# Attention startup: bias rows strided over partitions, a one-step maximum for the bias, first loads reordered

## The chip, the cores and the metric

The kernel runs on one core of a Trainium2 chip. The metric is the device time of one execution in microseconds. The kernel before takes 820.88 us (median of three runs, 820.48 to 823.38). Rows of the trace come from one profiled execution, which took 827.75 us, 826.0 of it between its first and last instruction (the span).

## The reference

Attention with a learned position bias, then two mixtures of experts. Only attention matters here; q, k and v have the shape (2 batches, 8 heads, 576 rows, 64).

```
scores = (q @ k^T) / 8
rel    = pos[:, None] - pos[None, :]
x      = log1p(|rel|) / log1p(max(pos_i, 1))        # 576 x 576
h      = max(x[..., None] @ w1 + b1, 0)             # 32 hidden units
bias   = h @ w2                                     # one 576 x 576 plane per head
attn   = softmax(scores + bias) ; out = attn @ v
```

The bias does not depend on the batch, so each row block of it serves both batches. The result is reshaped to 1152 tokens of 512 and goes through a dense mixture of 4 experts (every token, weighted by domain_probs) and a routed one of 8.

## The kernel before

**Tiles.** Attention is cut into nine units u: units 0 to 7 are 128 query rows of one batch (batch u % 2, rows from 128 * (u // 2)), unit 8 is the last 64 rows of both. A unit has eight heads; a step n is one head of one unit, n = 8 u + h, 72 steps in all. What is called head n below is the step with that n. The bias is made in five blocks of query rows (`blk`), four of 128 rows and one of 64 that is stored twice, for the two halves of unit 8; a block has eight pieces T of 16 rows (block 4 has four).

**A bias piece.** `bias_r` (L287) makes four row tiles r (tt = 0 to 3) of 128 x 576: the partitions are 4 query rows x 32 hidden units. Each is one instruction, on VectorE, ScalarE or GpSimd as the letters in `AT` and `RE` say: with log for the table `lm` of log1p(|rel|), shifted per row: max(log * w1 / psi_i, -b1) on VectorE and GpSimd, relu(log * w1 / psi_i + b1) on ScalarE; the constant that the first form leaves out is put back from `bconst`. `bias_mm` (L303) multiplies with a block-diagonal w2 on TensorE, `bias_out` (L315) evicts the two PSUM halves with ScalarE into bo (128 x 576: 16 rows x 8 heads) and SP sends bo to the 16 partitions 16 T to 16 T + 15 of the bias block; in block 4 two DMAs send it to both halves.

**Other helpers.** `load_q`, `load_k`, `load_v` issue loads on SP. `split` (L134) makes a high and a low part on GpSimd, two instructions; `k_split` and `split_q` use it. `q_trans` and `k_trans` transpose on TensorE, `k_out` (L203) copies a transposed k piece out of PSUM, q_trans's result is copied by ScalarE and then twice by SP (qt<-qt, 64 partitions each). `v_scale` finds a power of two for v of both batches, `v_mul` scales v, `v_hi` and `v_lo` split it.

**Order.** All is written out by hand inside `manual_schedule`: every engine and every DMA queue works in program order. L500 to L519: first loads, splits of q and k. L534 to L556: ten steps T that make block 0, with k's transposes of batch 0 and the first scores between. L557 to L568: splits of batch 1's k and three of its five passes `k_pass` (transposes and copies). From L574: steps n = -2 to 77, each with the transposes of head n, soft_max of head n + 2 on VectorE (L344), exp of head n + 1 on ScalarE (L354), the high part of the transposed e on ScalarE and the low part on VectorE, scores of head n + 3, and the product with v of head n - 2. Bias pieces of the next blocks are woven in (`group`); the last two k passes come in steps -2 and -1. Block 4's pieces are evicted from about n = 45 on.

**PSUM.** The transposes of e and of k share one pool of two buffers (`ps_et`).

Of the kernel before, what the change touches and what calls it, by code (L numbers as in the profile page):

```python
# [59 lines left out]

@with_exitstack
def attn_moe_moe_kernel(ctx, tc, q, k, v, w1, b1, w2, dp, mw1, mw2, wg, wog, ew1, ew2, cst, lmc, out):
# [173 lines left out]
    def v_scale(p, tag):  # L236
        pt = p.tile([128, 2, 128], F32, tag=tag, name="vtp")
        for b in range(2):
            dve.tensor_reduce(out=vmx[:, b:b + 1], in_=vt["raw"][:, b].rearrange("p n d -> p (n d)"), axis=AX.X, op=ALU.max,
                              apply_absolute_value=True)  # L240
            yield
        for b in range(2):
            pe.transpose(pt[0:1, b, :], vmx[:, b:b + 1], idn)
        dve.tensor_reduce(out=vma, in_=pt[0:1], axis=AX.X, op=ALU.max)
        pe.matmul(pt[:, 0, 0:2], lhsT=onr, rhs=vma, start=True, stop=True)
        yield
        dve.tensor_scalar(out=vP[:, 0:2], in0=pt[:, 0, 0:2], scalar1=1e-30, scalar2=None, op0=ALU.max)
        dve.tensor_scalar(out=vP[:, 0:2].bitcast(I32), in0=vP[:, 0:2].bitcast(I32), scalar1=0x7F800000, scalar2=None, op0=ALU.bitwise_and)
        dve.reciprocal(vR, vP[:, 0:2])
        for b in range(2):  # L250
            dve.tensor_copy(vP[64 * b:64 * b + 64, 2:3], vP[64 * b:64 * b + 64, b:b + 1])
        yield
# [1025 lines left out]
```

## Time and profile before

| | |
|---|---|
| median of three runs | 820.88 us |
| profiled execution, own time / span | 827.75 / 826.0 us |
| TensorE busy | 755.2 us (91%) |
| VectorE busy | 500.1 us (61%) |
| ScalarE busy | 470.2 us (57%) |
| GpSimd busy | 373.4 us (45%) |
| DMA | 160.18 MB, mean 194 GB/s |

In the rows further down PE is TensorE, DVE is VectorE, ACT is ScalarE, POOL is GpSimd and SPq is the queue of SyncE from which DMAs are issued. A name such as bias<-bo says what an instruction writes and reads; [3.51 <-DMA bias<-bo] says that the engine sat idle for 3.51 us and what ended that. The DMA share is the mean busy share of the core's 16 DMA engines and can go over 1 where packets overlap. [...]

### The profile page before, as it was taken

Reading aid. Unit: us, or ns where it says so; the run is one execution under the profiler, and the core shown is the slowest. Engines: PE = TensorE matmul, PEld = TensorE weight load, DVE = VectorE, ACT = ScalarE, POOL = GpSimd, SP = SyncE. Lnnn points to the kernel's source line nnn. Section 1 sums busy time; section 2 is a strip of 40 time slices with the busy share of each in tenths; the row PEclk is TensorE's granted clock in tenths of the full one; section 3 lists DMA queues with packets and bytes.
Section 4 is the critical chain, followed back from the end, with each engine's and each line's share of the span. In section 5 each row is a group of like instructions: output and inputs, shape, how many; then the busy total and the mean of one; then the engine's idle time right before and its main releaser. Section 6 shows DMA issues by size and latency. Waiting matters only on the chain. (4 is left out here: it accounts for less than half of the span.)

```text
span 826.0 us, 16298 instructions
## 1 busy us (share of the span) xinstructions
PE 755.2 (91%) x6305; PEld 482.9 (58%) x6305; DVE 500.1 (61%) x1120; ACT 470.2 (57%) x683; POOL 373.4 (45%) x265
## 2 busy tenths in 40 slices
PE   1777999997898999999999999999999789999994
PEld 0344777776786555555555555555555477667771
DVE  4979999986878565565555555554567373333220
ACT  1646899985674667667667667766663132222220
POOL 7737566562380555555555555555543103112110
PEclk9999999998999999999999999999999899999998
DMA  8944545599353567564846567573527738999340
GB/s 224 158 60 79 97 97 102 106 170 142 67 151 117 220 242 252 223 255 152 294 167 237 217 234 251 217 271 117 215 112 294 309 129 321 409 408 360 107 158 16
DMA packets 75039, 160.18 MB, mean 194 GB/s; under 512 B 20364, under 2 KB 28812, under 8 KB 74958
## 3 DMA queue, kind: packets, MB, share of 16 engines
q1 hardware_dynamic: 68832, 144.52, 55.7%
q0 software_dynamic: 4528, 14.47, 5.3%
q8 instruction: 51, 0.84, 0.4%
q10 hardware_dynamic: 1598, 0.11, 0.1%
q14 instruction: 30, 0.25, 0.1%
HBM read 116.32 MB, written 39.34 MB: 188 GB/s over the span
## 5 line engine op out<-in xcount | busy, mean ns | idle before, releaser
L494 POOL TENSOR_TENSOR ring<-wraw,ring 128x1024 f16<-128x1024 f32 x64 | 136.2, 2129 | 118.7 <-ACT wraw L491 102.6
L723 DVE SCALAR_TENSOR_TENSOR h<-hps,h 128x384 f16<-128x384 f32 x96 | 53.2, 557 | 146.4 <-ACT h L722 146.4
L718 PE MATMUL hps<-xt,wt 128*128 128x384 f16 x384 | 126.0, 328 | 2.2 <-DVE h L723 1.8
L720 PE MATMUL hps<-xt,wt 128*128 128x384 f16 x384 | 126.0, 328 | 0.0
L719 PE MATMUL hps<-xt,wt 128*128 128x384 f16 x384 | 126.0, 328 | 0.0
L459 DVE TENSOR_REDUCE wm<-wraw 128x1 f32<-128x1024 f32 x96 | 116.0, 1209 | 0.0
L491 ACT ACTIVATE wraw<-wraw,wR 128x1024 f32<-128x1024 f32 x91 | 104.5, 1148 | 3.0
L735 PE MATMUL yps<-wt,h 128*128 128x512 f16 x264 | 100.1, 379 | 0.0
L736 PE MATMUL yps<-wt,h 128*128 128x512 f16 x264 | 100.1, 379 | 0.0
L737 PE MATMUL yps<-wt,h 128*128 128x512 f16 x264 | 100.1, 379 | 0.0
L722 ACT ACTIVATE h<-hps 128x384 f16<-128x384 f32 x96 | 46.7, 487 | 88.5 <-PE hps L720 84.6
L494 POOL TENSOR_TENSOR wt<-wraw,wt 128x1024 f16<-128x1024 f32 x31 | 66.1, 2132 | 63.3 <-ACT wraw L491 63.0
L486 ACT ACTIVATE ring<-wraw,wR 128x1024 f16<-128x1024 f32 x64 | 73.0, 1141 | 21.5 <-DVE wR L475 18.8
L296 DVE TENSOR_SCALAR r<-lm,s,nb 128x576 f32<-128x576 f32 x89 | 75.8, 899 | 0.0
L335 PE MATMUL sc<-kt,qt 128*128 128x288 f32 x320 | 62.8, 321 | 13.6 <-DVE mn L344 7.3
L1036 PE MATMUL l<-xb,wb 128*128 128x128 f16 x1248 | 72.8, 219 | 2.5 <-DMA wb<-wdr 2.5
L1036 PEld LDWEIGHTS <-wb 128*128 128x128 f16 x1248 | 70.7, 98 | 6.4 <-DMA wb<-wdr 3.3
L1055 PE MATMUL l<-wb,xb 128*128 128x512 f16 x312 | 69.5, 379 | 0.8 <-ACT o L1059 0.8
L344 DVE CUSTOM_DVE_ANT_0 ns<-sc,bias 128x576 f32<-128x576 f32 x72 | 54.3, 754 | 24.6 <-PE sc L335 13.0
L1044 DVE SCALAR_TENSOR_TENSOR xb<-l,xb 128x512 f16<-128x512 f32 x26 | 17.6, 691 | 80.1 <-ACT xb L1043 80.1
L296 POOL TENSOR_SCALAR r<-lm,s,nb 128x576 f32<-128x576 f32 x20 | 45.7, 2285 | 42.7 <-PE bp L311 42.7
L1060 POOL DMA_INDIRECT out_x<-o,g x13 | 13.2, 1016 | 108.4 <-ACT o L1059 93.5
(246 smaller groups left out, 1459.2 us busy)
## 6 DMA issues: line engine op xcount, KB each, us to landing
wb<-wdr SPq DMA_DIRECT2D x104, 512.0 KB
wraw<-in_moe_w SPq DMA_DIRECT2D x84, 512.0 KB
wdr<-ring SPq DMA_DIRECT2D x64, 512.0 KB
bias<-bo SPq DMA_DIRECT2D x40, 288.0 KB
wraw<-in_moe_w POOLq DMA_DIRECT2D x12, 512.0 KB, 5.5
qt<-qt SPq DMA_DIRECT2D x40, 128.0 KB
ydr<-y POOLq DMA_DIRECT2D x9, 258.0 KB, 4.1
q<-in_q SPq DMA_DIRECT2D x8, 256.0 KB
```

The lines of the kernel that those rows point to most:

```text
L296: (dve if on == "v" else pool).tensor_scalar(out=r, in0=src, scalar1=sc, scalar2=nb1, op0=ALU.mult, op1=ALU.max)
L459: dve.tensor_reduce(out=wm[:, w_col(x), k:k + 1], in_=wraw[x][:, k], axis=AX.X, op=ALU.max, apply_absolute_value=True)
L486: act.activation(out=hi, in_=t, func=AF.Copy, scale=R)
L491: act.activation(out=t, in_=t, func=AF.Copy, scale=R)
L494: pool.tensor_tensor(out=lo, in0=t, in1=hi, op=ALU.subtract)
L718: pe.matmul(ps, lhsT=w[:, k, 0, fs], rhs=xt[:, c, 0, k, :], start=(k == 0), stop=False)
L719: pe.matmul(ps, lhsT=w[:, k, 0, fs], rhs=xt[:, c, 1, k, :], start=False, stop=False)
L720: pe.matmul(ps, lhsT=w[:, k, 1, fs], rhs=xt[:, c, 0, k, :], start=False, stop=(k == 3))
L735: pe.matmul(acc[m][t], lhsT=hh, rhs=w[:, f // 2, 0, ws], start=(f == 0), stop=False)
L736: pe.matmul(acc[m][t], lhsT=hh, rhs=w[:, f // 2, 1, ws], start=False, stop=False)
L737: pe.matmul(acc[m][t], lhsT=hl, rhs=w[:, f // 2, 0, ws], start=False, stop=(f == 7))
L1036: pe.matmul(ps[f // 4][:, f % 4, :], lhsT=w[:, k, a, f * 128:f * 128 + 128], rhs=xs[:, b, k, :], start=(k == 0 and f % 4 == 0 and i == 0), ...
```

## The change

**Rows strided.** Piece T of a block of 128 rows now holds rows T, T + 8, T + 16, ... instead of 16 adjacent rows (`row0`, and log1p's table shifted by 8 per group of rows), and one DMA writes every eighth partition from T on. In block 4 a piece goes out in four DMAs, each of 64 partitions of bo to eight partitions.

**One maximum.** log is multiplied by w1 once, in place (704 of its 1152 columns at the start, 448 after block 0). A row tile is then max(log * w1, -b1 * psi_i): one operation, with an accumulator output (`accum_out`) on VectorE and without on GpSimd; ScalarE adds a bias per partition. The factor 1 / psi_i moves to the eviction, as its scale operand.

**First loads.** w1, b1, w2's block-diagonal form, the reordered tables and domain_probs come from the host inside the constants; the first loads are log's 704 columns on SP and 342 columns of constants on ScalarE's queue, then q 0, k of batch 0 and two pieces of k of batch 1. The rest (`bulk`) follows one by one in the steps T.

**v and k.** v's factor is found per batch, without a transpose. v of batch 0 is loaded in the steps T, v of batch 1 behind block 0. v of batch 0 gets its high part from ScalarE, in steps -1 and 0. All five k passes of batch 1 run in steps -1 to 3, behind the product with v; all copies of them and more of batch 0's go to ScalarE. v of batch 1 is scaled in step 4.

```diff
+def row0(blk, T, tt):
+    return blk * 128 + T + 32 * tt if blk < 4 else 512 + 2 * T + tt // 2 + 32 * (tt % 2)
...
-        (dve.tensor_copy if x and not b else act.copy)(o, pt)
+        (dve.tensor_copy if x and not b and a < 2 else act.copy)(o, pt)
...
-        src, sc = lm[:, 575 - 4 * t:1151 - 4 * t], s1[:, t:t + 1]
-        if on != "a":
-            (dve if on == "v" else pool).tensor_scalar(out=r, in0=src, scalar1=sc, scalar2=nb1, op0=ALU.mult, op1=ALU.max)
+        r0 = row0(blk, T, tt)
+        src = lm[:, 575 - r0:1151 - r0]
+        if on == "v":
+            dve.tensor_scalar(out=r, in0=src, scalar1=nbp[:, t:t + 1], scalar2=None, op0=ALU.max, op1=ALU.max,
+                              accum_out=rmx[:, rb[1]:rb[1] + 1])
+        elif on == "p":
+            pool.tensor_scalar(out=r, in0=src, scalar1=nbp[:, t:t + 1], scalar2=None, op0=ALU.max)
         else:
-            act.activation(out=r, in_=src, func=AF.Relu, scale=sc, bias=b1c)
+            act.activation(out=r, in_=src, func=AF.Relu, bias=bps[:, t:t + 1])
...
-            act.activation(out=bo[:, z * 288:z * 288 + 288], in_=pt, func=AF.Identity, bias=bconst[:, w:w + 1])
-        for p0 in ([16 * T] if blk < 4 else [16 * T, 64 + 16 * T]):
-            sp.dma_start(out=bias_t[blk][p0:p0 + 16], in_=bo)
+            act.activation(out=bo[:, z * 288:z * 288 + 288], in_=pt, func=AF.Identity, bias=bconst[:, w:w + 1],
+                           scale=cs[:, C_INV + blk * 8 + T:C_INV + blk * 8 + T + 1])
+        if blk < 4:
+            sp.dma_start(out=bias_t[blk][T:128:8], in_=bo)
+            return
+        for x in range(2):
+            for p0 in (0, 64):
+                sp.dma_start(out=bias_t[blk][p0 + 2 * T + x:p0 + 64:8], in_=bo[64 * x:64 * x + 64])
...
-        act.dma_start(out=w1c, in_=rep4(w1, 1))
-        act.dma_start(out=b1c, in_=rep4(b1, 1))
-        sp.dma_start(out=cs, in_=cst[:, 0:C_N])
-        sp.dma_start(out=lm, in_=lmc)
-        act.dma_start(out=w2s, in_=rep4(w2, 8))
+        sp.dma_start(out=lm[:, 448:1152], in_=lmc[:, 448:1152])
+        act.dma_start(out=cs[:, 0:C_UT], in_=cst[:, 0:C_UT])
         load_q(0)
         for a in (0, 1, 2):
             load_k(0, a)
+        for a in (2, 0):
+            load_k(1, a)
...
+        dve.tensor_scalar(out=nbp, in0=cs[:, C_RP:C_RP + 144], scalar1=b1c, scalar2=-1.0, op0=ALU.mult, op1=ALU.mult)
+        act.activation(out=bps, in_=nbp, func=AF.Copy, scale=-1.0)
+        dve.tensor_scalar(out=lm[:, 448:1152], in0=lm[:, 448:1152], scalar1=w1c, scalar2=None, op0=ALU.mult)
...
+        bulk = [lambda: load_k(1, 1), lambda: load_q(1), lambda: load_v(0, 0), lambda: load_v(0, 1), lambda: load_v(0, 2),
+                lambda: sp.dma_start(out=lm[:, 0:448], in_=lmc[:, 0:448]), lambda: None, lambda: load_v(1, 0)]
...
-            if T in (5, 7):
-                next(vs)
-            if T == 8:
-                qk(0)
+        for a in (1, 2):
+            load_v(1, a)
...
-        k_pass(4, 0, 1)
...
             if n == -2:
+                v_scale(0)
                 v_mul(0)
-                for a in range(5):
-                    v_hi(0, a, pool)
-                    v_lo(0, a)
-                    if a == 2:
-                        split_q(1)
...
+            if n in (-1, 0):
+                for a in ((0, 1, 2), (3, 4))[n + 1]:
+                    v_hi(0, a, act)
+                    v_lo(0, a)
+                if n == 0:
+                    split_q(1)
...
-                    bias_r(1, n + 2, tt, "vvvv"[tt] if n == -1 else "vavv"[tt])
+                    bias_r(1, n + 2, tt, "vavv"[tt])
...
-                k_pass(n + 4)
...
+            if -1 <= n < 4:
+                k_pass((4, 0, 1, 2, 3)[n + 1])
+            if n in (1, 2):
+                v_max(1, n - 1)
             if n == 2:
+                v_pow(1)
+            if n == 4:
+                v_scale(1)
                 v_mul(1)
```

## Rows read from the trace of the kernel before

**Rows 1.** The page's 40 slices, TensorE's busy tenths.

```profile
PE   1777999997898999999999999999999789999994
```

**Rows 2.** Windows: length, busy us (instructions) of PE, PEld, DVE, ACT, POOL; PEclk, share, GB/s.

```profile
0.00:10.00 10.00, 0.00 (x0) 0.00 (x0) 0.45 (x2) 1.28 (x1) 4.19 (x14) 1.00 0.74 187
10.00:20.00 10.00, 2.99 (x12) 0.96 (x16) 7.53 (x10) 1.74 (x4) 9.69 (x9) 1.00 0.96 257
...
16.00:18.00 2.00, 0.63 (x4) 0.22 (x4) 2.00 (x2) 1.20 (x2) 1.92 (x2) 1.00 1.11 334
...
20.00:50.00 30.00, 24.02 (x188) 11.58 (x188) 28.76 (x34) 16.32 (x31) 16.51 (x13) 1.00 1.01 149
...
110.00:130.00 20.00, 19.95 (x257) 15.76 (x256) 18.77 (x42) 18.46 (x35) 11.87 (x8) 1.00 0.51 101
```

**Rows 3.** Timeline, GpSimd and VectorE at the start: start us, us, instruction, count.

```profile
3.54 0.29 POOL L510 CAST idb<-cs 128x128 bf16<-128x128 f32 x1 [2.64 <-DMA cs<-in_cst]
...
11.43 3.12 DVE L525 COPY w2b<-w2s 32x8 f32<-32x8 f32 x4 [2.17 <-DMA w2s<-in_w]
...
15.82 14.69 DVE L296 TENSOR_SCALAR r<-lm,s,nb 128x576 f32<-128x576 f32 x11
...
41.26 1.55 DVE L296 TENSOR_SCALAR r<-lm,s,nb 128x576 f32<-128x576 f32 x3
...
60.20 7.10 DVE L296 TENSOR_SCALAR r<-lm,s,nb 128x576 f32<-128x576 f32 x6
```

**Rows 4.** Timeline: last eviction of block 0 and the first soft_max (head 0).

```profile
46.12 0.89 ACT L320 ACTIVATE bo<-sc,bconst 128x288 f32<-128x288 f32 x2 [1.26 <-PE sc L311]
...
53.28 0.76 DVE L344 CUSTOM_DVE_ANT_0 ns<-sc,bias 128x576 f32<-128x576 f32 x1 [3.51 <-DMA bias<-bo]
```

**Rows 5.** Windows: the hole in the traffic, its end, and a qt transfer.

```profile
22.00:24.00 2.00, 1.27 (x7) 0.18 (x2) 2.00 (x3) 1.25 (x2) 1.92 (x3) 1.00 0.06 16
...
50.50:51.00 0.50, 0.50 (x4) 0.50 (x3) 0.00 (x0) 0.11 (x1) 0.00 (x0) 0.50 0.20 18
...
74.50:75.50 1.00, 0.95 (x15) 0.71 (x11) 1.00 (x4) 1.00 (x3) 0.63 (x1) 1.00 0.88 203
```

**Rows 6.** Timeline of VectorE: soft_max of heads 10, 18, 26, 42 and 58.

```profile
90.27 0.74 DVE L344 CUSTOM_DVE_ANT_0 ns<-sc,bias 128x576 f32<-128x576 f32 x1
...
109.78 0.76 DVE L344 CUSTOM_DVE_ANT_0 ns<-sc,bias 128x576 f32<-128x576 f32 x1
...
129.32 0.76 DVE L344 CUSTOM_DVE_ANT_0 ns<-sc,bias 128x576 f32<-128x576 f32 x1
...
168.39 0.76 DVE L344 CUSTOM_DVE_ANT_0 ns<-sc,bias 128x576 f32<-128x576 f32 x1
...
217.40 0.76 DVE L344 CUSTOM_DVE_ANT_0 ns<-sc,bias 128x576 f32<-128x576 f32 x1
```

**Rows 7.** The dip: a qt issue, the wait for it (timeline), and two windows.

```profile
185.95 0.50 SPq L165 DMA_DIRECT2D qt<-qt  x1
...
197.97 1.06 PE L335 MATMUL sc<-kt,qt 128*128 128x288 f32 x3 [4.23 <-DMA qt<-qt]
...
188.00:198.00 10.00, 5.75 (x76) 4.45 (x74) 5.77 (x12) 6.76 (x13) 4.57 (x3) 0.94 1.05 148
198.00:203.00 5.00, 5.00 (x37) 4.58 (x39) 2.04 (x6) 1.20 (x2) 0.00 (x0) 0.50 1.17 145
```

**Rows 8.** ScalarE's groups by form: shapes, count, busy us, mean ns; idle time before.

```profile
L354 ACT ACTIVATE e<-ns,mn 128x576 f32<-128x576 f32 x72 | 56.4, 783 | 0.3 <-DVE mn L344 0.2
L367 ACT ACTIVATE eth<-etp 128x512 f16<-128x512 f32 x72 | 43.2, 600 | 27.0 <-PE etp L361 27.0
L320 ACT ACTIVATE bo<-bp,bconst 128x288 f32<-128x288 f32 x64 | 30.2, 505 | 19.8 <-PE bp L311 18.1 <-issue 1.3
L298 ACT ACTIVATE r<-lm,b1c,s 128x576 f32<-128x576 f32 x35 | 30.2, 869 | 0.0
L209 ACT CAST kt<-ktp 128x512 fp32r<-128x512 f32 x12 | 7.2, 622 | 2.7 <-PE ktp L200 2.5
```

More of the change, by code (lines that the diff above doesn't have):

```diff
@@ L33 @@
 C_ID = 144
-C_UT = C_ID + 128
+C_W1 = C_ID + 128
+C_B1 = C_W1 + 1
+C_WB = C_B1 + 1
+C_INV = C_WB + 32
+C_UT = C_INV + 36
 C_IOTA = C_UT + 128
@@ L42 @@
 C_IOP = C_N
-C_ALL = C_IOP + 128
+C_DP = C_IOP + 128
+C_ALL = C_DP + 36
 NE = 3
@@ L234, in init_v, with v_max, v_pow, v_scale @@
             pool.memset(z[64 * e:64 * e + 64, :, :, 0, e, 64:65], 1.0)
[L236 to L252, printed above, removed]
+    def v_max(b, x):
+        raw = vt["raw"][:, b].rearrange("p (x n) d -> p x (n d)", x=2)
+        dve.tensor_reduce(out=vm2[:, x:x + 1], in_=raw[:, x], axis=AX.X, op=ALU.max, apply_absolute_value=True)
+    def v_pow(b):
+        m = vmx[:, b:b + 1]
+        dve.tensor_reduce(out=m, in_=vm2, axis=AX.X, op=ALU.max)
+        dve.tensor_scalar(out=m, in0=m, scalar1=1e-30, scalar2=None, op0=ALU.max)
+        dve.tensor_scalar(out=m.bitcast(I32), in0=m.bitcast(I32), scalar1=0x7F800000, scalar2=None, op0=ALU.bitwise_and)
+        dve.tensor_copy(vpb[:, b:b + 1], m)
+    def v_scale(b):
+        pt = ps_t.tile([128, 128], F32, tag="t", name="vpp")
+        pe.matmul(pt, lhsT=vpb[:, b:b + 1].to_broadcast([128, 128]), rhs=idb, start=True, stop=True)
+        dve.tensor_reduce(out=vP[:, b:b + 1], in_=pt, axis=AX.X, op=ALU.max)
+        dve.reciprocal(vR[:, b:b + 1], vP[:, b:b + 1])
+        dve.tensor_copy(vP[64 * b:64 * b + 64, 2:3], vP[64 * b:64 * b + 64, b:b + 1])
     def v_mul(b):
@@ L540, in attn_moe_moe_kernel @@
                     bias_r(0, T, tt, "a" if tt in AT[T % 2] else "v")
-            if 1 <= T < 9:
+            if T == 8:
+                for x in range(2):
+                    v_max(0, x)
+                v_pow(0)
+                qk(0)
+            if T:
                 bias_mm(0, T - 1)
                 bias_out(0, T - 1, len(AT[(T - 1) % 2]))
-            if 1 <= T < 4:
-                load_v(1, T - 1)
-            if T == 2:
+                bulk[T - 1]()
+            if T == 1:
                 q_trans(0, 0)
-            if 3 <= T < 8:
+            if 2 <= T < 7:
                 for g in range(2):
-                    k_trans(0, T - 3, g, ps_et, "et")
+                    k_trans(0, T - 2, g, ps_et, "et")
             if T == 4:
                 q_trans(0, 1)
-            if T in (5, 7):
-                next(vs)
-            if T == 8:
-                qk(0)
+        for a in (1, 2):
+            load_v(1, a)
+        sp.dma_start(out=cs[:, C_UT:C_N], in_=cst[:, C_UT:C_N])
+        dve.tensor_scalar(out=lm[:, 0:448], in0=lm[:, 0:448], scalar1=w1c, scalar2=None, op0=ALU.mult)
         for a in (4, 0, 1, 2, 3):
             k_split(1, a)
-        for _ in vs:
-            pass
         def k_pass(*pieces):
@@ L667, in attn_moe_moe_kernel @@
                 split_q(8)
-                dpr = dp.rearrange("(b t) e -> b t e", b=2)
-                for b in range(2):
-                    sp.dma_start(out=pr[:, b:8:2, :], in_=dpr[b, 0:512].rearrange("(k p) e -> p k e", p=128))
-                    sp.dma_start(out=pr[64 * b:64 * b + 64, 8, :], in_=dpr[b, 512:576])
+                sp.dma_start(out=pr, in_=cst[:, C_DP:C_DP + 36].rearrange("p (u e) -> p u e", e=4))
             if n == 70:
@@ L1226, in attn_moe_moe_kernel, with constants @@
                     pass
[L1229 removed]
+def constants(w1, b1, w2, dp):
     i = np.arange(S, dtype=np.float32)
     c = np.zeros((128, C_ALL), np.float32)
[L1232 to L1234 removed]
+    psi = np.log1p(np.maximum(i, np.float32(1.0)))
+    at = np.array([[row0(t // 32, t // 4 % 8, t % 4) + 8 * g for t in range(144)] for g in range(4)])
+    c[:, C_RP:C_RP + 144] = np.repeat(psi[at], 32, axis=0)
+    inv = (1.0 / psi)[at].reshape(4, 36, 4).transpose(2, 0, 1).reshape(16, 36)
+    c[:, C_INV:C_INV + 36] = np.repeat(inv, 8, axis=0)
+    c[:, C_ID:C_ID + 128] = np.eye(128)
+    for b in range(2):
+        d = dp.reshape(2, S, 4)[b]
+        c[:, C_DP:C_DP + 36].reshape(128, NU, 4)[:, b:8:2] = d[0:512].reshape(4, 128, 4).transpose(1, 0, 2)
+        c[64 * b:64 * b + 64, C_DP + 32:C_DP + 36] = d[512:576]
+    c[:, C_W1] = np.tile(w1.reshape(32), 4)
+    c[:, C_B1] = np.tile(b1.reshape(32), 4)
+    for g in range(4):
+        c[32 * g:32 * g + 32, C_WB + 8 * g:C_WB + 8 * g + 8] = w2
     c[:, C_UT:C_UT + 128] = np.triu(np.ones((128, 128)), 1)
```

56 lines of the change are left out of this document (19 added, 37 removed).

## The prediction

> **What bounds the kernel now.** I read the 40 slices first, then busy time in windows, then the timeline of the first 90 us. The PE line of the slices is full nearly everywhere except at its left edge and in a dip near 200 us [rows 1]; the windows say the same in numbers: TensorE is busy 19.95 of 20 us in the middle of attention [rows 2], so whatever only makes VectorE, ScalarE or GpSimd cheaper there is worth nothing. All that this change touches lies in two places: the time before attention runs at its own pace, and the dip.
>
> The pace: VectorE's soft_max of heads 18 and 26 start at 109.78 and 129.32, and head 10 at 90.27, 19.5 us before head 18 [rows 6]. So 19.54 us per 8 heads, and the kernel is "on the line" from head 10 on. What comes before is a startup of 90 us. Its hinge is the first soft_max (head 0) at 53.28: VectorE had stood idle 3.51 us, for the last DMA of the bias of block 0, although ScalarE had written that piece near 47.0 [rows 4]. The DMA engines were full: 1.01 share from 20 to 50 us at only 149 GB/s, against 257 from 10 to 20 [rows 2]. VectorE itself starts its bias rows only at 15.82, behind small loads (w2s came at 11.43) and 3.12 us of copies of w2 [rows 3], and then needs 14.69 us for 11 of them while GpSimd splits q and k; three of them take 1.55 us once GpSimd is idle [rows 3].
>
> **The change part by part.** All times are of the profiled execution (span 826.0, own time 827.75); the median of three runs is 820.88, so 6.9 us lower, and the difference is carried over at the end.
>
> *First loads and small copies.* Gone: three ScalarE DMAs and SP's load of all constants and all of lm (805 KB ahead of q), five VectorE copies, two GpSimd memsets. In their place 360 KB of lm (704 columns) on SP and 175 KB of constants on ScalarE's queue, side by side. The constants landed at 3.54 before, ahead of lm [rows 3]; I take 4.0 for both now, then nbp, the scaling of lm (704 columns, about as long as one bias row), w2r on GpSimd, the cp matmul and its two copies: first bias row at about 6, 10 us earlier.
>
> *Bias rows as one maximum.* The 24 VectorE rows of block 0 lose the multiplication and get an accumulator output. The trace has no such instruction. Bounds: 0.52 us (three in 1.55) and 1.34 us (11 in 14.69) [rows 3], the first without and the second with GpSimd at work. I take 0.70, near the soft_max instruction, which also writes an accumulator and is 0.76 long for the same 576 columns [rows 4], and which does not stretch. [...] 24 x 0.70 = 17 us, and two k copies: VectorE would be through the block at about 25. ScalarE has 8 rows of 0.87, 16 evictions of 0.505, eight copies of k of up to 0.62 (three of them taken over from VectorE) and two of q [rows 8]: 7 + 8 + 5 + 1 = 21 us, with its waits for the matmuls between, last eviction at about 28 (47.0 before). GpSimd's splits start about 1.5 us earlier than before, with q, and stay just ahead of the transposes. The scale operand on the eviction I cost at nothing: the instruction is the same.
>
> *DMA: what is ahead of the last bias piece.* Now the queue is late next. Ahead of the last piece lie: first loads (lm, constants, q 0, k of batch 0, two pieces of k of batch 1) 2583 KB; then the bulk loads spread over the steps (last k piece, q 1, v of batch 0, rest of lm) and four qt copies, 2661 KB; and eight bias pieces of 288 KB. Moved behind it: v of batch 1, 1152 KB. The first 10 us moved 1870 KB (187 GB/s) and after that 257 GB/s held [rows 2]: first loads through at 10 + 713/257 = 12.8, the rest another 10.4. A bias piece before: from 20 to 50.5 us, less the hole at 22 to 24 [rows 5], less 2166 KB of other data at 257 GB/s (8.4 us), 20.2 us for eight, 2.5 us each (115 GB/s). After, strided over partitions: nothing here writes 16 strided rows. Bounds: 2.5 us, and 1.1 us at 257 GB/s. I take 1.42, the rate of qt, which writes 64 partitions (203 GB/s at 0.88 share) [rows 5]; 8 x 1.42 = 11.4. Sum 12.8 + 10.4 + 11.4 = 34.6. From the end of traffic (50.5, [rows 5]) to the soft_max before there were 2.8 us; the same again gives head 0 at 37.4 instead of 53.3: **-16 us**. Bounds -7 (2.5 us a piece) and -22 (the queue keeps up and ScalarE's chain decides, 28 + 3 = 31). SP also issues the bulk loads behind evictions that it must wait for; since its backlog is never empty from 10 us on, I cost that at nothing; without the backlog it would be about 1 us.
>
> *From head 0 to the line.* Before, head 10 came 37.0 us after head 0 [rows 4, 6]. VectorE gets lighter: in step -1 six bias rows took 7.10 us [rows 3] and now five take 3.5; step -2 has four as before; some 4 us saved. ScalarE gets heavier: four of the k passes (two copies of 0.62 each [rows 8]), which ran before head 0 or in steps -2 and -1, now run one each in steps 0 to 3, and v's copies, that GpSimd made, in steps -1 and 0 (four like an exp of 0.78 or a little less, two of half the size). ScalarE's work by durations [rows 8]: step -1: exp 0.78, v 2.0, bias row 0.87, evictions 1.0, short k copies 0.7, together 5.4; likewise 5.1, 3.6, 4.1 and 4.0 in steps 0 to 3, 22.2 in all. Two evictions of 0.505 take 0.89 together [rows 4], so 0.12 goes off for each of the 36 instructions: 18 us, from the first evictions of block 1 at about +7 to +25, where step 4 begins. Added wait: the two transposes of a pass share two PSUM buffers with the transposes of e, so the second waits for a ScalarE copy or the next VectorE split; behind it on TensorE stand the next head's transposes, and ScalarE waits for those. A copy and half a pass of transposes, 0.8 us a pass, 4 us in all: step 4 at +29, and four heads more at 2.44 bring head 10 to +39: **+2 us**. Bounds: -3 (VectorE's gain alone counts) and +6 (the wait costs twice that). v of batch 1 is scaled in step 4 instead of 2; GpSimd has six steps for its halves until head 8's product needs them.
>
> *The dip.* Head 42 to head 58 took 49.0 us where two periods are 39.1 [rows 6]. [...] Block 3's pieces get quicker, so less stands in the queue when block 4 begins. But block 4's four steps issue four DMAs of 144 KB to eight partitions each instead of two of 288 KB. I take **-3 us**, between 0 (block 4 as slow as before) and -8 (no wait, no slow clock). [...]
>
> *At nothing:* block rows on TensorE's line (GpSimd's shorter rows, VectorE's fixed 0.70: TensorE covers them), the long reductions of v in halves (VectorE waits for the queue then anyway), four loads of domain_probs as one.
>
> Sum: -16 + 2 - 3 = -17. 827.75 - 17 = 810.7 profiled; 820.88 - 17 = **804**, own range 798 to 809.
>
> **Rivals.**
> 1. *The engines decide, not the queue.* Loads moved at 334 GB/s for two us [rows 2], and full queues may beat 257; then head 0 is at 31 (-22), and the dip closes (-8): -22 + 2 - 8 = -28, 793. For it: my queue has no slack to lose; against: it did not hold that rate before: 257 is the mean of the ten us around it.
> 2. *The spread k and v become the new wait.* The passes cost +6 in place of +2, bias pieces 1.8 us (head 0 at 40, -13), the dip stays: -7, 814. For it: ScalarE and the two PSUM buffers; against: the steps were bound by VectorE before, which is relieved.
> [...]
> 4. *The maximum does not do what it says:* VectorE's rows still stretch to 1.34 beside GpSimd. Block 0 then ends at 6 + 32 + 2, head 0 at about 43 (-10), and the next two steps keep their length (+4): with the dip -9, 812.
>
> **How the numbers follow.** Forecast 0.50, rival 1 0.20, rival 2 0.18, rival 3 0.05, rival 4 0.04; 0.03 for no change to be measured. Range 792 to 815: it holds the forecast, rivals 1, 2 and 4, and leaves out the slower cases and the far ends of the faster. 0.5% is 4.1 us, about what can be told from no change: faster 0.91, same 0.04, slower 0.05.
>
> **What would show it.** First bias row on VectorE near 6 us, each about 0.7 and equally long beside GpSimd; last eviction of block 0 near 28; DMA share full from 2 to 35 us; head 0 near 37 with VectorE waiting for a bias DMA; head 10 about 39 us later; head 58 less than 49 us after head 42. Wrong if head 0 comes after 45, if ScalarE's copies of k hold steps 0 to 3 longer than 5 us each, or if a qt copy in block 4 is waited for longer than 4 us.

## The result, and the profile after

The changed kernel takes **814.69 us** (median of 8 runs, 811.81 to 816.91), the kernel before 820.84 (median of 8 beside them, 819.23 to 824.65): ratio 0.9903, 95% interval 0.9877 to 0.9929. A second set of runs (after_again below) gave 812.55 beside 823.67: 0.9862, interval 0.9817 to 0.9908. So the change is worth 6 to 11 us, where 17 were forecast: the direction held, the size did not, and the range (792 to 815) held the median by its last 0.3 us.

The profiled execution took 816.86 us (span 815.1). TensorE, its granted clock (PEclk, a share of full speed) and the DMA engines in the page's 40 slices: against [rows 1] TensorE's left edge has filled, but a hole has opened in its second slice (20 to 41 us), and the clock falls in the second and third (to 0.7 and 0.6).

```profile
PE   6477999998889999999999999999999789999994
...
PEclk9769999999999999999999999999999899999998
DMA  9912443466274386466647468564537739999340
```

Windows of the changed kernel, with the columns of [rows 2]:

```profile
0.00:10.00 10.00, 2.62 (x15) 1.32 (x17) 3.79 (x10) 3.17 (x6) 7.20 (x15) 1.00 0.95 212
...
12.00:14.00 2.00, 2.00 (x19) 0.81 (x17) 1.78 (x6) 1.45 (x3) 2.00 (x2) 1.00 0.35 65
20.00:40.00 20.00, 9.01 (x94) 4.79 (x92) 11.46 (x29) 11.33 (x22) 11.64 (x11) 0.77 1.14 217
...
30.00:42.00 12.00, 0.46 (x2) 0.28 (x3) 4.71 (x10) 2.04 (x4) 1.95 (x2) 0.54 1.04 201
42.00:48.00 6.00, 4.65 (x21) 1.99 (x21) 5.99 (x16) 0.59 (x1) 0.00 (x0) 0.50 0.12 28
52.00:58.00 6.00, 5.96 (x42) 3.64 (x38) 1.79 (x5) 4.68 (x10) 2.76 (x4) 0.50 0.20 52
110.00:130.00 20.00, 19.93 (x268) 15.83 (x267) 19.23 (x52) 18.63 (x35) 9.45 (x7) 1.00 0.43 106
```

The middle of attention is as full as before. From 30 to 42 us TensorE worked for 0.46 us and ScalarE for 2.04, while the DMA engines were full (share 1.04). From 20 to 40 us the DMA engines are as full as in [rows 2], at 217 GB/s instead of 149. The timeline answers [rows 3, 4]: first bias row at 7.09, the next 0.74 us later, last eviction of block 0 over at 30.6.

```profile
7.09 0.81 DVE L305 TENSOR_SCALAR_CACHE_REDUCE r<-lm,nbp 128x576 f32<-128x576 f32 x1
7.83 0.08 DVE L305 DVE_READ_ACCUMULATOR r<-lm,nbp 128x1 f32 x1
7.83 0.81 DVE L305 TENSOR_SCALAR_CACHE_REDUCE r<-lm,nbp 128x576 f32<-128x576 f32 x1
...
29.52 1.07 ACT L332 ACTIVATE bo<-bp,bconst,cs 128x288 f32<-128x288 f32 x2 [0.38 <-PE bp L323]
```

And the soft_max of heads 0, 2, 3, 6, 7, 10, 42 and 58 on VectorE, the clock of this case, against [rows 4, 6]:

```profile
41.01 0.76 DVE L361 CUSTOM_DVE_ANT_0 ns<-sc,bias 128x576 f32<-128x576 f32 x1 [2.64 <-DMA bias<-bo]
...
50.82 0.76 DVE L361 CUSTOM_DVE_ANT_0 ns<-sc,bias 128x576 f32<-128x576 f32 x1
...
57.03 0.76 DVE L361 CUSTOM_DVE_ANT_0 ns<-sc,bias 128x576 f32<-128x576 f32 x1 [3.30 <-PE sc L352]
...
70.66 0.76 DVE L361 CUSTOM_DVE_ANT_0 ns<-sc,bias 128x576 f32<-128x576 f32 x1 [1.58 <-ACT e L371]
...
77.32 0.75 DVE L361 CUSTOM_DVE_ANT_0 ns<-sc,bias 128x576 f32<-128x576 f32 x1
...
85.66 0.76 DVE L361 CUSTOM_DVE_ANT_0 ns<-sc,bias 128x576 f32<-128x576 f32 x1
...
164.44 0.75 DVE L361 CUSTOM_DVE_ANT_0 ns<-sc,bias 128x576 f32<-128x576 f32 x1
...
207.57 0.76 DVE L361 CUSTOM_DVE_ANT_0 ns<-sc,bias 128x576 f32<-128x576 f32 x1
```

Head 0 comes 12.3 us earlier than in [rows 4], head 10 only 4.6 earlier than in [rows 6]: **7.7 us are given back between them**. Heads 0 to 2 are 4.1 shorter than before; heads 2 to 3 take 4.5 more, 3 to 6 take 4.0 more, 6 to 7 take 4.4 more. Two places in the same timeline show how. In step -1 ScalarE makes three copies of v ahead of a bias row, and TensorE's product waits for that row; in step 4 VectorE waits for the small product of v's scale, which stands behind the output products on TensorE, and then multiplies v, with the soft_max of head 7 queued behind both:

```profile
49.21 1.65 ACT L269 CAST v<-vraw 128x512 f16<-128x512 f32 x3
50.76 0.77 ACT L310 ACTIVATE r<-lm,bps 128x576 f32<-128x576 f32 x1
...
51.58 2.14 PE L323 MATMUL bp<-r,cs 128*32 128x288 f32 x14 [2.21 <-ACT r L310]
...
75.03 0.22 PE L257 MATMUL vpp<-idb,vpb 128*128 128x128 bf16 x1
75.28 0.29 DVE L258 TENSOR_REDUCE vP<-vpp 128x1 f32<-128x128 f32 x1 [2.20 <-PE vpp L257]
...
75.99 1.42 DVE L264 TENSOR_SCALAR vraw<-vraw,vR 128x2304 f32<-128x2304 f32 x1
```

### The profile page after: what moved, and what is told of

It is laid out like the page before. It is cut to its first block, busy times and chain, and to the rows that moved or that the text cites. A ratio compares the mean times of both kernels' runs of the same rounds, so it can differ in the third digit from the quotient of the medians.

```text
span 815.1 us, 16401 instructions
## 1 busy us (share of the span) xinstructions
PE 750.1 (92%) x6303; PEld 481.3 (59%) x6303; DVE 488.5 (60%) x1210; ACT 476.2 (58%) x694; POOL 351.7 (43%) x258
## 3 DMA queue, kind: packets, MB, share of 16 engines
q1 hardware_dynamic: 67904, 144.38, 52.6%
## 5 line engine op out<-in xcount | busy, mean ns | idle before, releaser
L305 DVE TENSOR_SCALAR_CACHE_REDUCE r<-lm,nbp 128x576 f32<-128x576 f32 x88 | 67.0, 806 | 1.4 <-PE bp L323 1.3
L371 ACT ACTIVATE e<-ns,mn 128x576 f32<-128x576 f32 x72 | 56.5, 784 | 1.2 <-DVE mn L361 1.1
```

## The experiments

All kernels but before and before_again start from the changed kernel. They are read by stretches, from soft_max to soft_max as above. Most of these repeat from execution to execution within some tenths of a us, while the code behind the last head, the same in all, took between 571.7 and 577.9 us. Not all do: b4_adjacent, whose edit does not reach the first heads, has 4.4 from head 2 to head 3 at a granted clock of 1.00 (52 to 58 us) where the changed kernel has 6.0 and 6.2, in the profile with 6.2 at 0.50. The two profiles of the kernel before differ by 4.2 from head 42 to head 58, where the clock is at half from 198 to 203 us in one of them alone, and by 1.4 from head 3 to head 6, for which no row here shows a cause. All in us:

| kernel | head 0 | 0 to 2 | 2 to 3 | 3 to 6 | 6 to 7 | 7 to 10 | 0 to 10 | 42 to 58 | median |
|---|---|---|---|---|---|---|---|---|---|
| before, first profile | 53.3 | 13.9 | 1.8 | 9.6 | 2.3 | 9.4 | 37.0 | 49.0 | 820.8 |
| before_again | 52.6 | 13.9 | 1.8 | 11.0 | 2.3 | 9.4 | 38.4 | 44.8 | 823.1 (one run) |
| changed, first profile | 41.0 | 9.8 | 6.2 | 13.6 | 6.7 | 8.3 | 44.7 | 43.1 | 814.7 |
| after_again | 40.6 | 9.8 | 6.0 | 13.5 | 6.7 | 8.4 | 44.3 | 41.4 | 812.6 |
| k_first | 40.6 | 9.8 | 3.3 | 12.0 | 5.3 | 8.4 | 38.9 | 42.1 | 808.7 |
| warm | 40.8 | 9.8 | 5.2 | 13.6 | 6.7 | 8.3 | 43.6 | 41.6 | 816.0 |
| v_pool | 41.4 | 9.8 | 2.9 | 13.0 | 6.7 | 8.0 | 40.3 | 41.2 | 813.2 |
| adjacent | 48.2 | 9.8 | 4.4 | 13.7 | 6.7 | 8.3 | 42.9 | 43.0 | 824.9 |
| kv | 41.2 | 9.8 | 1.8 | 10.8 | 5.3 | 8.4 | 36.1 | 41.5 | 805.8 |
| late_kq | 38.6 | 9.8 | 5.7 | 14.2 | 6.7 | 8.3 | 44.6 | 42.7 | 814.1 |
| b4_adjacent | 40.4 | 9.8 | 4.4 | 13.7 | 6.7 | 8.2 | 42.8 | 46.2 | 817.8 |
| v_early | 41.4 | 8.0 | 5.1 | 13.8 | 4.5 | 8.0 | 39.3 | 42.3 | 811.1 |
| v1_late | 38.9 | 9.8 | 6.1 | 16.4 | 6.7 | 8.3 | 47.3 | 42.6 | 816.0 |
| no_acc | 42.4 | 7.4 | 7.6 | 13.9 | 6.7 | 9.8 | 45.3 | 43.0 | 816.9 |
| kv_early | 40.5 | 8.0 | 1.8 | 10.8 | 4.4 | 9.0 | 34.0 | 42.1 | 805.0 |
| q1_hole | 39.8 | 9.8 | 6.2 | 13.6 | 6.7 | 8.3 | 44.6 | 43.0 | 813.7 |
| best | 40.4 | 6.6 | 3.0 | 10.8 | 4.4 | 8.0 | 32.7 | 42.3 | 802.9 |

The medians of the experiments come from four sets, each on another chip, so they are compared with the kernel before of the same set (824.3 for k_first to adjacent, 823.7 for after_again to b4_adjacent, 823.6 for v_early to kv_early, 822.7 for the last two and before_again). Most single edits move the whole time by less than the intervals can tell; that is why the stretches decide.

**Between the heads.** k_first, warm, v_pool, kv and v_early.

```diff
# k_first
+        k_pass(4, 0, 1, 2, 3)
         NT = NU * NH
...
-            if -1 <= n < 4:
-                k_pass((4, 0, 1, 2, 3)[n + 1])
```

> The changed kernel, with all five k passes of batch 1 ahead of the first step instead of one in each of steps -1 to 3. In the changed kernel TensorE stands idle from 29.9 to 41.8 us and ScalarE from 30.6 to 41 but for two bias rows, and GpSimd's splits of k end at 32.0; so the passes fit there. Theory (the startup's gain is given back between head 0 and head 10, in the steps that took up the k passes, part of it through the half clock after the idle): head 0 stays near 41, the granted clock stays at 1.00 past 42, head 0 to head 10 falls from 44.7 us to 37 or less, time 7 to 9 us less, about 806. Rival (the queue and the late head 0 are all of the miss; the steps to head 10 are as long as their other work): head 10 at 84 to 86, time within 2 us of the changed kernel.

Measured: ratio to the kernel before 0.9818 (0.9745 to 0.9891); head 0 unmoved, head 0 to head 10 5.8 us shorter (5.5 against after_again). The passes fit into TensorE's idle stretch and cost nothing there. The rival falls. But not all of it is the passes: in this execution the clock did not fall again from 52 to 58 us (1.00, 0.50 in the changed kernel). Against b4_adjacent, which keeps the passes and has no second fall either, head 0 to head 10 is 3.9 shorter. What was expected of the clock failed: it was at 0.50 behind head 0 all the same.

```profile
42.00:48.00 6.00, 4.74 (x22) 1.96 (x21) 6.00 (x14) 0.96 (x2) 0.00 (x0) 0.50 0.08 20
```

```diff
# warm
+        warm = ps_et.tile([128, 512], F32, tag="et", name="warm")
+        for _ in range(11):
+            pe.matmul(warm, lhsT=idn, rhs=lm[:, 575:1087], start=True, stop=True)
         NT = NU * NH
```

> The changed kernel, with 11 further matmuls of 512 fp32 columns, whose product nobody reads, on TensorE between the last bias product of block 0 and the first step; all else in place. Rival theory C (the half clock alone costs the time between head 0 and head 10): granted clock 1.00 from 31 to 58, the products of block 1's bias 1.2 us for 16 instead of 3.5, head 0 to head 10 4 to 6 us shorter, time 4 to 6 us less. Theory W (the work of ScalarE and the k passes decides): under 2 us. If the matmuls run past 41 us they cost what they overlap.

Measured: 0.9896 (0.9825 to 0.9967), head 0 to head 10 shorter by 1.0 and 0.7 us. The clock, by windows of this kernel, stayed at 1.00 as long as the matmuls ran and fell again behind them:

```profile
31.00:42.00 11.00, 8.30 (x23) 3.66 (x22) 4.18 (x13) 1.44 (x2) 0.92 (x1) 1.00 0.96 196
42.00:50.00 8.00, 6.12 (x25) 2.44 (x24) 8.00 (x20) 2.78 (x5) 0.34 (x1) 0.58 0.12 28
54.00:58.00 4.00, 4.00 (x30) 2.55 (x29) 2.19 (x6) 3.05 (x6) 2.78 (x4) 0.63 0.28 74
```

So it did not test the half clock behind head 0. (Its second fall is a shorter one, and head 2 to head 3 is 5.2.) That stretch is answered by VectorE's busy time: 5.99 of 6 us in the changed kernel from 42 to 48, where TensorE runs at half clock. VectorE's own line sets heads 0 to 2, and head 0 to head 2 is 9.8 us in every kernel that does not change VectorE's work there. In no_acc (below), where VectorE's rows are shorter and the clock is again at 0.50 from 42 to 48 us, it is 7.4.

```diff
# v_pool
-                    v_hi(0, a, act)
+                    v_hi(0, a, pool)
```

> The changed kernel, with the rounded copies of v of batch 0 in steps -1 and 0 on GpSimd, as in the kernel before, instead of ScalarE. Theory V (the three copies of 1.65 us on ScalarE stand ahead of the bias row that TensorE's products wait 2.21 us for): head 2 to head 3 shrinks from 6.2 us by 1.6 to 2.5 and head 0 to head 1 to 2 is unchanged, time 1.5 to 3 us less. Theory C (clock): no more than 0.5 us.

Measured: 0.9860 (0.9789 to 0.9931). Head 2 to head 3 shrank by 3.2 to 3.3 us, twice what the copies themselves take. In this kernel's timeline ScalarE's bias row follows exp at once, and TensorE's 16 products run through:

```profile
48.89 0.76 ACT L371 ACTIVATE e<-ns,mn 128x576 f32<-128x576 f32 x1
49.56 0.76 ACT L310 ACTIVATE r<-lm,bps 128x576 f32<-128x576 f32 x1
...
49.55 1.99 PE L323 MATMUL bp<-r,cs 128*32 128x288 f32 x16
...
52.00:58.00 6.00, 5.40 (x48) 3.93 (x46) 4.63 (x10) 4.98 (x11) 5.62 (x7) 1.00 0.19 51
```

Without the wait the second fall of the clock is gone too (1.00 from 52 to 58, where the changed kernel has 0.50). The two can be told apart by b4_adjacent (below), which runs the same code as the changed kernel up to head 42. There ScalarE's copies stand ahead of the bias row as well, and TensorE waits 1.77 us for it, but in that execution the clock stayed up; heads 2 and 3, and the clock:

```profile
50.26 0.75 DVE L360 CUSTOM_DVE_ANT_0 ns<-sc,bias 128x576 f32<-128x576 f32 x1
...
54.67 0.76 DVE L360 CUSTOM_DVE_ANT_0 ns<-sc,bias 128x576 f32<-128x576 f32 x1 [2.00 <-ACT v L269]
...
52.00:58.00 6.00, 4.93 (x49) 3.50 (x46) 3.41 (x8) 5.72 (x12) 3.74 (x5) 1.00 0.20 52
```

So of the 3.2 to 3.3 us, 1.5 are the copies (4.4 to 2.9) and 1.6 to 1.8 the second fall of the clock (6.0 and 6.2 to 4.4). Theory V holds for the copies, at the lower end of what it expected; theory C has the rest.

> The changed kernel with both: the five k passes ahead of the first step, and v's copies of batch 0 on GpSimd. Alone the first took head 0 to head 10 from 44.7 to 38.9 and the second to 40.3. Theory (both add work to ScalarE and TensorE in the same steps and each is worth its own waits): 36 to 37, time 803 to 806. Rival (they remove the same waits, and VectorE's own work decides then): 38 to 39, time 807 to 809.

Measured (both edits above): 0.9773 (0.9726 to 0.9820), 805.8 beside 812.6 for the changed kernel in the same set. Head 0 to head 10 36.1, as the theory had it; head 2 to head 3 is back at the 1.8 us of before. Its runs (803.6 to 806.2) lie below all of the changed kernel's in this set (812.3 to 813.0).

```diff
# v_early: v_scale without its matmul, which is now v_pp
+        v_pp(0)
+        v_scale(0)
+        v_mul(0)
         NT = NU * NH
...
-            if n == -2:
-                v_scale(0)
-                v_mul(0)
...
+            if n == 4:
+                v_pp(1)
             if live(n + 3):
                 qk(n + 3)
```

> The changed kernel, with v's scale and product of batch 0 (0.28 + 0.16 + 0.13 + 1.42 us on VectorE) ahead of the first soft_max, where VectorE waits 2.64 us for the last bias piece, instead of behind it; and in step 4 the small product that v's scale of batch 1 waits for ahead of the next head's scores on TensorE instead of behind the output products (VectorE waited 2.20 us for it, with soft_max of head 7 queued behind). Theory (these stand in VectorE's line between the heads): head 0 to head 1 from 5.5 to 3.5, head 6 to head 7 from 6.7 to 4.4, head 0 to head 10 some 4 us shorter, time 808 to 810 beside 812.5. Rival (TensorE and ScalarE are late anyway in these steps): each gains under 0.7 us and the time stays within 1.5 us.

Measured: 0.9831 (0.9779 to 0.9883). Head 0 to head 2 1.8 us shorter, head 6 to head 7 2.1, head 0 to head 10 5.0 to 5.3: the theory, stretch by stretch. The whole moved less: 811.1, and its profiled execution took 575.4 us behind the last head, after_again's 573.5.

**The queue ahead of head 0.** adjacent, late_kq, v1_late and q1_hole.

```diff
# adjacent
-            sp.dma_start(out=bias_t[blk][T:128:8], in_=bo)
+            sp.dma_start(out=bias_t[blk][16 * T:16 * T + 16], in_=bo)
```

> The changed kernel, with each bias piece of blocks 0 to 3 written to 16 adjacent partitions instead of 16 partitions with a stride of 8; the rows land in the wrong order, so the bias is permuted. Theory (the stride makes the packet of 2304 bytes quick, some 180 ns against 280 to 385 before): head 0 moves from 41 to 47 to 50, the traffic of block 3 runs late into block 4 again, time 7 to 12 us more. Rival (packets were long because all queues were mixed, whatever the partitions): head 0 within 1.5 us, time within 2 us.

Measured: 1.0006 (0.9978 to 1.0033): without the stride no gain in the time is left. Its first soft_max:

```profile
48.19 0.76 DVE L361 CUSTOM_DVE_ANT_0 ns<-sc,bias 128x576 f32<-128x576 f32 x1 [2.38 <-DMA bias<-bo]
```

7.2 to 7.6 us later for eight pieces, so the stride takes 0.9 us off a piece of 288 KB. The packet records of the traces say the same: from 20 to 53 us a packet of 2304 bytes took 179 ns in the median in the changed kernel, 261 in this one and 281 in the kernel before. The theory holds at head 0; its second half, block 3's traffic in block 4, does not: head 42 to head 58 stayed at 43.0.

```diff
# late_kq
-        bulk = [lambda: load_k(1, 1), lambda: load_q(1), lambda: load_v(0, 0), lambda: load_v(0, 1), lambda: load_v(0, 2),
+        bulk = [lambda: None, lambda: None, lambda: load_v(0, 0), lambda: load_v(0, 1), lambda: load_v(0, 2),
...
+        load_k(1, 1)
+        load_q(1)
         for a in (1, 2):
             load_v(1, a)
```

> The changed kernel with the second k piece and q of batch 1 (512 and 256 KB) loaded behind the last bias piece of block 0 instead of in its second and third step. Theory (head 0 waits for what lies ahead of the last bias piece in the DMA queues, which moved near 190 GB/s): 768 KB less ahead, head 0 at 36.5 to 37.5 instead of 41.0, and the time 3 to 4.5 us less if the steps behind keep their length. Rival (VectorE's maximum of v or the evictions decide, or the queue runs empty earlier and gains nothing): head 0 at 39.5 or later, time within 1.5 us.

Measured: 0.9886 (0.9841 to 0.9932). Head 0 at 38.6: 2.0 to 2.4 us for 768 KB, about half of what was expected, between theory and rival; the whole time did not gain from it (814.1 beside 812.6 for the changed kernel in the same set). The DMA share fell to 0.56 from 16 to 18 us in this kernel: with less to load, SP's queue ran dry between the evictions.

```diff
# v1_late
-                lambda: sp.dma_start(out=lm[:, 0:448], in_=lmc[:, 0:448]), lambda: None, lambda: load_v(1, 0)]
+                lambda: sp.dma_start(out=lm[:, 0:448], in_=lmc[:, 0:448]), lambda: None, lambda: None]
...
-        for a in (1, 2):
-            load_v(1, a)
-        sp.dma_start(out=cs[:, C_UT:C_N], in_=cst[:, C_UT:C_N])
...
                 bias_out(1, n + 2, 1)
+                if n == -2:
+                    for a in range(3):
+                        load_v(1, a)
+                    sp.dma_start(out=cs[:, C_UT:C_N], in_=cst[:, C_UT:C_N])
```

> The changed kernel, with the loads of v of batch 1 and the last constants issued behind the first bias piece of block 1 (near 48 us) instead of right behind the last bias piece of block 0 (31.8 us). About 0.8 MB more had been moved when that piece landed than stood ahead of it in order of issue. Theory (loads issued behind a bias piece take their share of the engines, so it does not come before them): head 0 at 37 to 38 instead of 41. Rival (one or two of the 16 engines have more of the work, and the piece waits for these whatever is behind it): head 0 within 1 us of 40.6 to 41.0. The time: head 0's gain, less up to 2 us if v of batch 1 is late for its maximum in steps 1 and 2.

Measured: 0.9910 (0.9877 to 0.9943); head 0 of this kernel:

```profile
38.91 0.76 DVE L361 CUSTOM_DVE_ANT_0 ns<-sc,bias 128x576 f32<-128x576 f32 x1 [0.81 <-DMA bias<-bo]
```

It came 1.7 to 2.1 us earlier: what is issued behind a bias piece does delay it, though by half of what was expected. VectorE's chain over v's maximum ended only 0.81 us before, so little more was to be had. The time was lost again: v of batch 1 came late, and head 3 to head 6 took 2.8 to 2.9 us more.

```diff
# q1_hole
         for a in (2, 0):
             load_k(1, a)
+        load_q(1)
...
-        bulk = [lambda: load_k(1, 1), lambda: load_q(1), lambda: load_v(0, 0), lambda: load_v(0, 1), lambda: load_v(0, 2),
+        bulk = [lambda: load_k(1, 1), lambda: None, lambda: load_v(0, 0), lambda: load_v(0, 1), lambda: load_v(0, 2),
```

> The changed kernel, with q of batch 1's first block (256 KB) issued with the first loads instead of in the third step of block 0. From 12 to 14 us the DMA share falls to 0.35, since SP's queue waits for the first eviction with nothing left to issue. Theory (the hole is queue time lost to the last bias piece, about 1.3 us): head 0 at 39.6 to 40, 1 us less than 40.6 to 41.0. Rival (the queues fill up again behind the hole in any case, or the last piece waits for few of the engines): head 0 within 0.4 us. The time: within 1.5 us of the changed kernel.

Measured: 0.9889 (0.9856 to 0.9922). The hole has closed,

```profile
12.00:14.00 2.00, 2.00 (x23) 0.97 (x22) 1.68 (x6) 1.55 (x4) 2.00 (x2) 1.00 0.84 173
```

and head 0 came at 39.8, 0.9 to 1.3 us earlier. The theory holds; in the whole time it cannot be seen.

**The dip.** before_again, after_again and b4_adjacent.

> The kernel before once more, unchanged, for a second profile of it. The first had head 0 at 53.3, head 10 at 90.3, head 42 to head 58 in 49.0 us. Expected, if these are the kernel's and not one execution's: head 0 within 1 us, head 0 to head 10 37 within 1.5, head 42 to head 58 47 to 51. If the dip were 45 or less here, the 5.9 us that the changed kernel gained there would be in part the chance of one execution.

> The changed kernel once more, unchanged, beside the experiments and on their chip: what its time and its stretches are worth from one execution to the next. Expected: head 0 at 41.0 within 0.5, head 0 to head 10 44.7 within 1, head 42 to head 58 43 within 1.5; ratio to the kernel before 0.985 to 0.993. If the half clock were a matter of the single execution, head 0 to head 10 would differ by 2 us or more.

The kernel before, second profile, heads 0, 10, 42 and 58:

```profile
52.59 0.76 DVE L344 CUSTOM_DVE_ANT_0 ns<-sc,bias 128x576 f32<-128x576 f32 x1 [3.58 <-DMA bias<-bo]
...
90.95 0.74 DVE L344 CUSTOM_DVE_ANT_0 ns<-sc,bias 128x576 f32<-128x576 f32 x1
...
169.09 0.76 DVE L344 CUSTOM_DVE_ANT_0 ns<-sc,bias 128x576 f32<-128x576 f32 x1
...
213.86 0.76 DVE L344 CUSTOM_DVE_ANT_0 ns<-sc,bias 128x576 f32<-128x576 f32 x1
```

The startup repeats, the dip does not: 44.8 here, 49.0 in [rows 6], and 41.4 and 43.1 in the changed kernel. From 197 to 203 us the clock was at 1.00 in this profile, where [rows 7] has 0.50. So the dip's gain is between 1.6 and 7.7 us, 3.4 by the second pair of profiles and 5.9 by the first.

```diff
# b4_adjacent
-        for x in range(2):
-            for p0 in (0, 64):
-                sp.dma_start(out=bias_t[blk][p0 + 2 * T + x:p0 + 64:8], in_=bo[64 * x:64 * x + 64])
+        for p0 in [16 * T, 64 + 16 * T]:
+            sp.dma_start(out=bias_t[blk][p0:p0 + 16], in_=bo)
```

> The changed kernel with block 4's bias pieces written as before, by two DMAs of 288 KB to 16 adjacent partitions each, instead of four of 144 KB to 8 strided ones; the rows land in the wrong order in block 4. Block 3's stride made no difference to head 42 to head 58 (43.0 with adjacent rows in blocks 0 to 3, 43.1 without). Theory (block 4's own DMAs closed the dip): head 42 to head 58 back to 47 to 49, time 4 to 6 us more. Rival (VectorE's lighter rows, or the place of the clock's drop in one execution, did it): 42 to 44.5, time within 1.5 us.

Measured: 0.9921 (0.9894 to 0.9947), 5 us over the changed kernel of the same set. Head 42 to head 58 46.2, a little under what was expected, and TensorE waits for a qt copy again as in [rows 7], with the DMA engines full:

```profile
188.82 1.06 PE L351 MATMUL sc<-kt,qt 128*128 128x288 f32 x3 [3.18 <-DMA qt<-qt]
...
184.00:194.00 10.00, 6.82 (x75) 5.34 (x67) 5.16 (x16) 4.27 (x8) 0.07 (x1) 0.83 1.13 132
```

The same window of the changed kernel:

```profile
184.00:194.00 10.00, 9.06 (x115) 6.66 (x111) 8.77 (x23) 6.08 (x12) 2.31 (x3) 1.00 0.65 129
```

Nearly the same rate (129 and 132 GB/s) at 0.65 instead of 1.13 share: block 4's own strided DMAs closed the dip.

**VectorE's row.** no_acc, kv_early and best.

```diff
# no_acc
-            dve.tensor_scalar(out=r, in0=src, scalar1=nbp[:, t:t + 1], scalar2=None, op0=ALU.max, op1=ALU.max,
-                              accum_out=rmx[:, rb[1]:rb[1] + 1])
+            dve.tensor_scalar(out=r, in0=src, scalar1=nbp[:, t:t + 1], scalar2=None, op0=ALU.max)
```

> The changed kernel, with VectorE's bias rows as the maximum without the accumulator output; all results are the same. Theory (the form with the accumulator is the one that GpSimd does not stretch): the rows of block 0 take 1.2 to 1.35 us each beside GpSimd instead of 0.73, the last row of block 0 ends near 37 instead of 27.7, head 0 at 45 to 48, time 4 to 7 us more. Rival (the maximum alone, without the product, does not stretch either): 0.5 to 0.75 a row, head 0 within 1 us, and 0.2 us less for each of VectorE's rows beside the heads, time 0 to 3 us less.

Measured: 0.9898 (0.9845 to 0.9951). Nine rows beside GpSimd and four with GpSimd idle:

```profile
7.17 11.16 DVE L305 TENSOR_SCALAR r<-lm,nbp 128x576 f32<-128x576 f32 x9
...
44.94 1.80 DVE L305 TENSOR_SCALAR r<-lm,nbp 128x576 f32<-128x576 f32 x4
```

The changed kernel with GpSimd idle:

```profile
43.55 0.81 DVE L305 TENSOR_SCALAR_CACHE_REDUCE r<-lm,nbp 128x576 f32<-128x576 f32 x1
...
44.28 0.81 DVE L305 TENSOR_SCALAR_CACHE_REDUCE r<-lm,nbp 128x576 f32<-128x576 f32 x1
```

1.24 us against 0.45 for the plain form, and 0.73 from start to start with the accumulator in either place. The rows did stretch as the theory said, and block 0 ended on VectorE at 36.6 instead of 27.7; but head 0 moved only to 42.4: the last eviction ended at 38.4 instead of 30.6, and the DMA engines, which are full in the changed kernel, were not (share 0.68 from 30 to 42 us, 1.04 there). Beside the heads the plain form is the shorter one while GpSimd is idle (head 0 to head 2 7.4 instead of 9.8) and the longer one where GpSimd works (head 7 to head 10 9.8 instead of 8.3).

> The k passes ahead of the first step, v's copies of batch 0 on GpSimd, and v's scales early as in the first kernel of this set, all in one. Alone or together they gave head 0 to head 10 of 36.1 (the first two) and are expected to give 4 less for the third. Theory (independent waits): 32 to 33 us, time 801 to 803. Rival (the first steps are bound by VectorE's bias rows and by TensorE by then): 35 to 36, time 804 to 806.

Measured (the edits of kv and v_early together): 0.9757 (0.9707 to 0.9807). Head 0 to head 10 34.0, 2.1 less than kv, where the third edit alone gave 5.0 to 5.3 (3.4 against b4_adjacent): some of its gain lay in waits that the others take away too. VectorE now works without a break from 38.6 to 49.8.

```diff
# best: kv_early and q1_hole, and four columns of bconst for the rows' constants
-                    bias_r(1, n + 2, tt, "vavv"[tt])
+                    bias_r(1, n + 2, tt, ("aaav", "vaav")[n + 2][tt])
...
-                bias_out(1, n + 2, 1)
+                bias_out(1, n + 2, n + 4)
```

> The k passes ahead of the first step, v's copies on GpSimd, v's scales early, q of batch 1 with the first loads, and in the first two steps three of VectorE's bias rows (0.73 each) on ScalarE, which stands idle from 38 to 44.7 us there. In the kernel without the last two, VectorE worked without a break from 38.6 to 49.8 us. Theory (VectorE's rows set the first two steps by now): head 0 to head 2 from 8.0 to 5.8 us, head 0 to head 10 31.5 to 32.5, time 801 to 804. Rival (TensorE's products of the rows, at half clock there, take their place): head 0 to head 2 7.3 to 8, time 804 to 806.

Measured: **802.87** (6 runs, 800.81 to 806.42), ratio 0.9771 (0.9735 to 0.9806). Heads 0, 2 and 10:

```profile
40.35 0.76 DVE L364 CUSTOM_DVE_ANT_0 ns<-sc,bias 128x576 f32<-128x576 f32 x1 [0.80 <-DMA vraw<-in_v]
...
46.91 0.75 DVE L364 CUSTOM_DVE_ANT_0 ns<-sc,bias 128x576 f32<-128x576 f32 x1
...
73.03 0.76 DVE L364 CUSTOM_DVE_ANT_0 ns<-sc,bias 128x576 f32<-128x576 f32 x1
```

Head 0 to head 2 fell from 8.0 to 6.6, of which 1.2 were lost again from head 2 to head 3: between theory and rival. Head 0 itself waits for a load of v here, whose scaling now stands ahead of it, so q1_hole's gain does not show. It beats the kernel before and the changed kernel; kv, kv_early and best can't be told apart by their intervals.

## Why the prediction missed

In both pairs of profiles the sum can be set out term by term (first pair, second pair): head 0 -12.3, -12.0; head 0 to head 10 +7.7, +6.0; head 10 to head 42 +0.7, +0.6; head 42 to head 58 -5.9, -3.4; the rest -1.1, -1.2. Together -10.9 and -10.0 in the span. The first set's median fell by 6.2 only: the first profile of the kernel before was 6.9 us over its median, that of the changed kernel 2.2. Part of this is the dip, 4.2 us longer in that profile than in before_again; the forecast took its base from it.

1. **From head 0 to the line: forecast +2, measured +6.0 to +7.7. This step failed.** VectorE's gain of 4 us was right (head 0 to head 2 13.9 to 9.8). So were the passes: put at 0.8 us each, 4 in all, they are 3.9 when k_first is set against b4_adjacent, where the clock does not fall a second time either (5.5 to 5.8 against the changed kernel, where it does), and 4.2 when kv is set against v_pool. Three things were not in the sum. The copies of v stood only in ScalarE's sum of busy time, as if it did not matter where they stand: ahead of the bias row they cost 1.5 us between heads 2 and 3 (1.6 by kv against k_first). The clock's second fall, from 51 to 58 us, for which the sum has no term, cost 1.6 to 1.8 more there; it came in both profiles of the changed kernel and not in b4_adjacent, so it is partly chance. And v's scale of batch 1 in step 4, costed at nothing, stands between heads 6 and 7, which take 4.4 us more: VectorE waited 2.2 for a product of 0.22 us that stood behind the output products (v_early took 2.1 away, k_first 1.3), and then multiplied v for 1.42, which the kernel before does two steps earlier. Undone one at a time (k_first, v_pool, v_early) the three give 5.6, 4.2 and 5.2 us (the last with 1.8 from the scale of batch 0); together (kv_early) they give 10.5, not 15. Against b4_adjacent they are 3.9, 2.5 and 3.4, together 8.8: most of what they seemed to share is the one fall of the clock, which k_first and v_pool took away (1.00 from 52 to 58 us) and v_early, with 5.1 from head 2 to head 3, seems to have shortened. What is left then is 3.0 to 4.4 less than before, VectorE's gain alone, which was the forecast's lower bound.
2. **DMA, head 0: forecast -16, measured -12.0 to -12.3.** The gain of a piece was sized nearly right: 2.5 less 1.42 is 1.08 us by the forecast, 0.9 by adjacent, 7.2 to 7.6 us in place of 8.6 for all eight. Two other sentences failed. "Its backlog is never empty from 10 us on": it ran empty from 12 to 14, for 0.9 to 1.3 us (q1_hole). And v of batch 1 "moved behind it" was not out of the way, for 1.7 to 2.1 us (v1_late). If the two add up (they were not run together), they are 2.6 to 3.4 of the 3.2 to 3.6 by which head 0 came after the forecast's 37.4. With the eight pieces that is more than was missed, so they overlap, or another term was put too high; this stays open.
3. **The dip: forecast -3, measured -3.4 and -5.9.** Right within what repeats, but not for the reason given: block 3's pieces did nothing (adjacent), block 4's did it (b4_adjacent).
4. **Bias rows: forecast 0.70, equal beside GpSimd (an estimate from the 0.76 of soft_max in [rows 4]); measured 0.73, equal.** Right. **First row at 6, last eviction near 28:** 7.1 and 30.6, with the queue deciding either way.
5. **The scale operand on the eviction, costed at nothing, was not free:** 505 ns in [rows 8], 598 after,

```profile
L332 ACT ACTIVATE bo<-bp,bconst,cs 128x288 f32<-128x288 f32 x66 | 36.1, 598 | 17.6 <-PE bp L323 11.7 <-issue 4.3 <-DMA bias<-bo 1.5
```

0.09 us on each of the block evictions; no run here took it away, so what it costs in the end is open.

Of the rivals, the second ("the spread k and v become the new wait", 814) came closest by its time (814) and by what it made the new wait, the spread work of k and v: +6 in place of +2, head 0 at 40. The passes alone, to which it gave the +6, cost what the forecast had; the copies and the scale of v and the clock made up the rest. Its dip was wrong, and its reason for head 0, slower pieces, is at most a part of it. The first fell (the queue still decides head 0), and so did the third, the slower kernel: the stride brought head 0 from 48.2 (adjacent) to between 40.6 and 41.0, and no run shows block 4's smaller strided DMAs taking longer: with them head 42 to head 58 took 43.1 and 41.4 us, against 46.2 with the adjacent ones (b4_adjacent) and 49.0 and 44.8 before. The fourth fell too (the rows do not stretch: 0.73 with and without GpSimd). Open stay how the terms at head 0 share what was missed there, and what varies behind the last head.
